# An attention, a router and two dense layers in one kernel: own tiles for the halves of a pair, weight splits moved, the halo of v copied on the chip

## The chip, the core and the metric

The kernel runs as one launch on one core of a Trainium2 chip. The metric is the device time of one execution in microseconds. A core has a matrix engine (TensorE, in the profile PE, its weight loads PEld), a vector engine (VectorE, DVE), a scalar engine (ScalarE, ACT), GpSimd (POOL) and SyncE (SP), which issues most DMA transfers. Each engine takes its instructions strictly in order, and engines wait for one another by semaphores.

## The reference

What is computed, cut to its core (float32 throughout):

```python
# 1. attention: batch 4, 8 heads, 576 positions, 64 per head; window 32.
#    heads 0-3: rel in [0, 32); heads 4-7: rel in [0, 128) and rel % 4 == 0
attn = softmax(where(mask, q @ k.T / 8, -1e9)); x = attn @ v      # -> 2304 x 512
# 2. router: 8 experts of exactly 288 tokens each, greedy by the sorted logits
logits = x @ w_gate                                                # 2304 x 8
out[assigned == e] = relu(x[assigned == e] @ w1[e]) @ w2[e]        # 512 -> 1024 -> 512
# 3. gated layer: 512 -> 1536 -> 512
y = (sigmoid(out @ w_gate2) * (out @ w_val)) @ w_out
```

## The kernel before, in words

The program has four stages, one behind the other on TensorE: the attention, the routing, the eight experts (`phase_m`) and the gated layer (`phase_g`).

**Attention.** The dilated heads are permuted on the host so that they too see a plain window of 32. There are four phases (head kind and batch pair), each of nine blocks of 64 queries: 36 groups, taken two at a time as 18 pairs, here p0 to p17. A block needs its 64 queries, and 96 keys and values: its own 64 and the 32 ahead of them, the halo. The host lays v out with the halo repeated, so that a block of v has 96 rows. `steps` writes the order of the work out by hand. In the turn of pair p stand: loads of the next phase (`load`, on SP's queue), the scores of p (`scores`, TensorE), the transposes of the exponentials of p-1 (`pt`: two halves of four transposes, each half followed by a copy from PSUM on ACT), the router's products of p-3 (`logit`, in the two phases of the plain heads), `norm` and the transposes `xt` of p-2 (DVE, TensorE), the products with v of p-1 (`av`), and the row maximum, subtraction and exponential of p (`soft`: DVE, DVE, ACT). The last pair is taken in halves. The rows of x go to DRAM (`rows_out`, SP). Numbers n in the program count half turns: n = 2p and 2p+1.

Both halves of `pt` write one PSUM tile of two banks and one SBUF tile:

```python
if g == 0:
    self.st[p, "pt"] = (self.ps_t.tile([128, 8, 128], ...), self.sp.tile([KEYS, 8, 128], ...))
...
nc.scalar.copy(t[:, j], ps[0:KEYS, j])
```

**Weights of the experts.** `fetch` loads 512 KB of float32 weights into one of four `raw` buffers. `high` (ACT) rounds them to the upper part, `low` (DVE) subtracts that to get the lower part; both parts lie in a ring of five. The first three splits stand in the attention, at n = 28, 30 and 32, and seven fetches at n = 22 to 25 and 33 to 35.

**Routing.** `settle` searches a threshold for each expert in five steps (DVE and TensorE in turn, with products that keep TensorE busy, `warm`), writes the row numbers (`rows`), starts the gathers of x on GpSimd, and passes a branch on a flag that all engines read. Behind it `tokens` writes `toks`, and the pools of the routing are closed. Then `turn` transposes the gathered rows (tile `xps`), and splits them into `xh` (ACT) and `xl` (DVE); the first product of the experts (tile `hps`) needs both, and the two parts of the weights.

A DMA of SP waits until the eighth DMA ahead of it has landed, so that up to eight are under way.

Of the kernel before, what the change touches and what calls it, by code (L numbers as in the profile page):

```python
# [65 lines left out]
def lay_v(v):  # L66
    a = kinds(v).transpose(0, 1, 5, 2, 3, 4, 6)
    a = np.concatenate([a, np.ones(a.shape[:-1] + (1,), a.dtype)], -1).reshape(2, 2, S, VW)
    a = np.concatenate([np.zeros((2, 2, HALO, VW), a.dtype), a], 2)
    return np.ascontiguousarray(np.stack([a[:, :, QB * i:QB * i + KEYS] for i in range(NBLK)], 3))  # L70


class Attn:
# [3 lines left out]
    def __init__(self, tc, ctx, qh, kh, vh, wgate, cst, xrows, L, LT):  # L77
# [6 lines left out]
        self.ps_s, self.ps_o, self.ps_t, self.ps_x = (p(n, 1, space=PS) for n in ("ps_s", "ps_o", "ps_t", "ps_x"))  # L84
# [10 lines left out]
    def zeros(self, eng):  # L95
        for k in self.k:
            eng.memset(k[:, 0], 0.0)

    def load(self, f, part, what="qkv"):
# [46 lines left out]
    def soft(self, p):  # L146
        nc, V = self.nc, self.nc.vector
        ps = self.st.pop((p, "s"))
        mx = self.sp.tile([128, 2, 4], F32, tag="mx", name="mx")
        d = self.sp.tile([128, 4, 2, KEYS], F32, tag="d", name="d")  # L150
        e = self.sp.tile([128, 8, KEYS], F32, tag="e", name="e")
        for gs in self.halves(p):
            n = 2 * len(gs)
            j = slice(2 * gs[0], 2 * gs[0] + n)
            V.tensor_reduce(out=mx[:, :, j], in_=ps[:, :, j], axis=AX.X, op=ALU.max)
            V.tensor_tensor(out=d[:, j].rearrange("p j h k -> p h j k"), in0=ps[:, :, j],
                            in1=mx[:, :, j].unsqueeze(3).to_broadcast([128, 2, n, KEYS]), op=ALU.subtract)
            nc.scalar.activation(out=e[:, 4 * gs[0]:4 * gs[0] + 2 * n].rearrange("p j k -> p (j k)"), in_=d[:, j].rearrange("p j h k -> p (j h k)"),
                                 func=AF.Exp, scale=0.125)
        self.st[p, "e"] = e  # L160
# [12 lines left out]
    def av(self, p, g):  # L173
        nc = self.nc
        t = self.st[p, "pt"][1]
        if g == 0:
            self.st[p, "o"] = self.ps_o.tile([128, 2, 512], F32, tag="o", name="o")
        o = self.st[p, "o"]
        f, i = self.groups[2 * p + g]
        v = self.v[f % 2][:, i].rearrange("p (b h c) -> p b h c", b=2, h=4)  # L180
        for h in range(4):
            for b in range(2):
                out = slice(64 * b, 64 * b + 64)
                nc.tensor.matmul(o[out, g, 65 * h:65 * h + 65], t[:, 4 * g + h, out], v[:, b, h], start=True, stop=True)

    def norm(self, p, gs=(0, 1)):
        V = self.nc.vector
        o = self.st[p, "o"][:, :, 0:260].rearrange("p g (h c) -> p g h c", h=4)
        if gs[0] == 0:
            self.st[p, "r"] = self.sp.tile([128, 2, 4], F32, tag="r", name="r")  # L190
            self.st[p, "x"] = self.xp.tile([128, 2, 4, 64], F32, tag="x", name="x")
        g = slice(gs[0], gs[-1] + 1)
        r, x = self.st[p, "r"][:, g], self.st[p, "x"][:, g]
        V.tensor_scalar(out=r, in0=o[:, g, :, 64], scalar1=1e-9, scalar2=None, op0=ALU.add)
        V.reciprocal(r, r)
        V.tensor_tensor(out=x, in0=o[:, g, :, 0:64], in1=r.unsqueeze(3).to_broadcast([128, len(gs), 4, 64]), op=ALU.mult)
        for k in gs:
            self.rows_out(2 * p + k, self.st[p, "x"][:, k].rearrange("p h d -> p (h d)"))
# [19 lines left out]
    def xt(self, p, gs=(0, 1)):  # L218
        nc = self.nc
        x = self.st[p, "x"].rearrange("p g (r h) d -> p g r (h d)", r=2)  # L220
        pool, n = (self.ps_t, 1024) if gs == [1] else (self.ps_x, 512)
        ps = pool.tile([128, n], F32, tag="t" if n > 512 else "x", name="xt")[:, 0:512].rearrange("p (r b g q) -> p r b g q", r=2, b=2, g=2)
        for g in gs:
            for r in range(2):
                nc.tensor.transpose(ps[:, r, :, g], x[:, g, r], self.cst["id"])
        self.st[p, "xt", gs[0]] = ps

    def xts(self, p, gs=(0, 1)):
        copy = self.nc.scalar.copy
# [4 lines left out]
        if plain:  # L234
            if (p, "xts") not in self.st:
                self.st[p, "xts"] = self.sp.tile([128, 2, 2, 128], F32, tag="xts", name="xts")
            t = self.st[p, "xts"]
            g = slice(plain[0], plain[-1] + 1)
            copy(t[:, g].rearrange("p g r (b q) -> p (r b) g q", b=2), ps[:, :, :, g].rearrange("p r b g q -> p (r b) g q"))
# [13 lines left out]
    def logit(self, p, gs=(0, 1), out=None):  # L253

        nc = self.nc
        for g in gs:
            f, i = self.groups[2 * p + g]
            kind, bp = self.phases[f]
            if kind:
                continue  # L260
            t, d = self.st[p, "xts"], self.xd
            xs = [t[:, g, r] for r in range(2)] + [d[:, i, r].rearrange("p b j r -> p (b j r)") for r in range(2)]
            j, k = divmod(i, 4)
            for w in (2, 3, 0, 1):
                dst = self.LT[:, 128 * j:128 * j + 128] if out is None else out
                nc.tensor.matmul(dst[32 * w:32 * w + 32], self.wr[:, k, w], xs[w],
                                 start=k == 0, stop=k == 3 or i == NBLK - 1)
# [4 lines left out]
    def fold(self, js):  # L272
        for j in js:
            n = min(4, NBLK - 4 * j)
# [3 lines left out]
    def steps(self):  # L278
        N = len(self.groups) // 2
        A = self.nc.scalar.copy  # L280
        for p in range(N):
# [13 lines left out]
            if p >= 1:  # L295
                self.av(p - 1, 0)
                self.av(p - 1, 1)
            self.soft(p)
            if p >= 2:
                self.xts(p - 2)  # L300
            if p == 12:
                self.spill(slice(0, 384), A)
                self.fold(range(3))
# [27 lines left out]
        self.fold(range(2, 3))  # L331
# [59 lines left out]
class Route:  # L391
# [180 lines left out]
    def settle(self, rows, gather, segments=(5, 1, 2)):  # L572
# [7 lines left out]
        with self.tc.block():  # L580
# [5 lines left out]
            with self.tc.If(v > 0, label="settled"):  # L586
# [3 lines left out]
                gather()  # L590

# [421 lines left out]
def program(tc, top, qh, kh, vh, wgate, cst, csb, wm, wgv, out):  # L1013
    nc = tc.nc
    with tc.manual_schedule():
# [12 lines left out]
        mring = ExitStack()  # L1028
        dn.ring = pool(mring, "ring", 5, side="right")
        with ExitStack() as rt:  # L1030
# [6 lines left out]
            with ExitStack() as at_ctx:  # L1037
# [8 lines left out]
                nc.scalar.activation(out=rows.bitcast(F32)[:, 0:1], in_=nc.const_aps.tensor(1.0, [128, 1], F32), func=AF.Exp)  # L1046
# [89 lines left out]
```

## Time and profile before

| what | value |
|---|---|
| median of three runs | 833.12 us (832.93 to 835.58) |
| the profiled execution's own time | 834.7 us, span 832.9 us |
| attention | 0 to 122.2 us: TensorE busy 90.9 us |
| routing up to `rows` | 122.2 to 156.1 us |
| branch, gather, transposes | 156.1 to 164.7 us |
| experts and gated layer | 164.7 to 832.9 us: TensorE busy 661.6 of 668.2 us |
| DMA share, 0 to 41.5 us | 0.90 of 16 engines, 227 GB/s |

Times of rows count from the span's start. The busy share of TensorE over the span (94%) says little of the attention, where each engine waits for others in every turn. A wait in brackets is the engine's idle time just ahead of the row and what ended it; "issue" there means that no semaphore was waited for.

### The profile page before, as it was taken

Reading aid. Unit: us, or ns where it says so; the run is one execution under the profiler, and the core shown is the slowest. Engines: PE = TensorE matmul, PEld = TensorE weight load, DVE = VectorE, ACT = ScalarE, POOL = GpSimd, SP = SyncE. Lnnn points to the kernel's source line nnn. Section 1 sums busy time; section 2 is a strip of 40 time slices with the busy share of each in tenths; the row PEclk is TensorE's granted clock in tenths of the full one; section 3 lists DMA queues with packets and bytes.
Section 4 is the critical chain, followed back from the end, with each engine's and each line's share of the span. In section 5 each row is a group of like instructions: output and inputs, shape, how many; then the busy total and the mean of one; then the engine's idle time right before and its main releaser. Section 6 shows DMA issues by size and latency. Waiting matters only on the chain.

```text
span 832.9 us, 14224 instructions
## 1 busy us (share of the span) xinstructions
PE 786.3 (94%) x5873; PEld 720.1 (86%) x5873; DVE 436.7 (52%) x747; ACT 303.3 (36%) x534; POOL 49.5 (6%) x72
## 2 busy tenths in 40 slices
PE   8688578799999999999999999999999999999996
PEld 5566454499999999999999999999999999999996
DVE  4455358556677766666654543445655543333322
ACT  3445330155565555544432433332322222212210
POOL 1030000311001100000000000000000000111002
PEclk9899799999999999999999999999999999999999
DMA  9879540256666666535312221112222101121002
GB/s 251 203 222 258 166 144 1 68 167 231 208 242 226 236 235 220 198 111 192 127 48 86 71 79 41 45 45 89 70 65 100 39 20 39 57 76 39 24 14 76
DMA packets 41278, 100.56 MB, mean 121 GB/s; under 512 B 4296, under 2 KB 20328, under 8 KB 41208
## 3 DMA queue, kind: packets, MB, share of 16 engines
q1 hardware_dynamic: 38088, 89.89, 34.2%
q0 software_dynamic: 2976, 9.54, 3.3%
q8 instruction: 48, 0.79, 0.4%
q10 hardware_dynamic: 144, 0.16, 0.1%
q14 instruction: 22, 0.18, 0.1%
HBM read 85.42 MB, written 14.16 MB: 120 GB/s over the span
## 4 chain that ended last, share of the span: by engine, by line
PE 78%; DMA 1%; ACT 1%; DVE 0%; POOLq 0%; POOL 0%; issue 0%; SPq 0%; ACTq 0%
PE gv L923 35%; PE o L945 18%; PE hps L805 12%; PE y L827 12%; PE xps L782 1%; DMA raw<-in_moe_dram 1%; ACT yo L831 0%; ACT L927 0%; POOLq L1132 0%; POOL out_dram L959 0%; DVE acc L957 0%; DVE xl L793 0%; ACT cm L746 0%; ACT xh L792 0%; PE y L847 0%
## 5 line engine op out<-in xcount | busy, mean ns | idle before, releaser
L923 PE MATMUL gv<-yhi,gw 128*128 128x384 f32 x1152 | 305.2, 336 | 0.3 <-ACT sg L927 0.3
L923 PEld LDWEIGHTS gv<-yhi,gw 128*128 128x128 f32 x1152 | 209.3, 188 | 3.7 <-ACT sg L927 0.6
L923 PE MATMUL gv<-ylo,gw 128*128 128x384 f32 x576 | 193.0, 335 | 0.0
L928 DVE TENSOR_TENSOR sg<-sg,gv 128x384 f32<-128x384 f32 x72 | 39.8, 552 | 186.0 <-PE gv L923 186.0
L945 PE MATMUL o<-gw,ghi 128*128 128x512 f32 x432 | 134.4, 392 | 0.0
L923 PEld LDWEIGHTS gv<-ylo,gw 128*128 128x128 f32 x576 | 108.1, 188 | 3.0
L728 DVE TENSOR_TENSOR wlo<-raw,whi 128x1024 fp32r<-128x1024 f32 x64 | 78.3, 1224 | 45.5 <-ACT whi L723 44.9
L931 ACT CAST ghi<-sg 128x384 fp32r<-128x384 f32 x72 | 36.9, 513 | 162.5 <-DVE sg L928 162.5
L945 PEld LDWEIGHTS o<-gw,ghi 128*128 128x128 f32 x432 | 80.1, 188 | 13.4
L927 ACT ACTIVATE sg<-gv 128x384 f32<-128x384 f32 x72 | 35.4, 492 | 144.6 <-PE gv L923 144.3
L945 PE MATMUL o<-gw,glo 128*128 128x512 f32 x216 | 85.4, 396 | 0.0
L805 PE MATMUL hps<-xh,whi 128*128 128x288 f32 x256 | 77.0, 301 | 0.0
L805 PE MATMUL hps<-xh,wlo 128*128 128x288 f32 x256 | 75.9, 297 | 0.0
L827 PE MATMUL y<-hh,wlo 128*128 128x288 f32 x256 | 75.6, 295 | 0.0
L827 PE MATMUL y<-hh,whi 128*128 128x288 f32 x256 | 75.5, 295 | 0.0
L827 PE MATMUL y<-hl,whi 128*128 128x288 f32 x256 | 75.4, 295 | 0.0
L805 PE MATMUL hps<-xl,whi 128*128 128x288 f32 x256 | 75.0, 293 | 0.0
L723 ACT CAST whi<-raw 128x1024 fp32r<-128x1024 f32 x64 | 66.8, 1043 | 8.0 <-DMA raw<-in_moe_dram 8.0
L932 DVE TENSOR_TENSOR glo<-sg,ghi 128x384 fp32r<-128x384 f32 x72 | 40.2, 559 | 41.7 <-ACT ghi L931 41.7
L809 ACT ACTIVATE hh<-hps 128x288 fp32r<-128x288 f32 x64 | 26.4, 412 | 69.8 <-PE hps L805 69.8
L805 PEld LDWEIGHTS hps<-xl,whi 128*128 128x128 f32 x256 | 48.4, 189 | 0.1
L827 PEld LDWEIGHTS y<-hl,whi 128*128 128x128 f32 x256 | 48.4, 189 | 0.0
(139 smaller groups left out, 994.6 us busy)
## 6 DMA issues: line engine op xcount, KB each, us to landing
raw<-in_moe_dram SPq DMA_DIRECT2D x100, 512.0 KB
raw<-yd SPq DMA_DIRECT2D x28, 384.0 KB
v<-in_v_dram SPq DMA_DIRECT2D x12, 390.0 KB
yd<-yo SPq DMA_DIRECT2D x8, 576.0 KB
q<-in_q_dram SPq DMA_DIRECT2D x12, 256.0 KB
k<-in_k_dram SPq DMA_DIRECT2D x12, 256.0 KB
v<-in_v_dram SPq DMA_DIRECT2D x4, 585.0 KB
xrows<-x SPq DMA_DIRECT2D x18, 128.0 KB
```

The source lines that it names most:

```text
L723: self.nc.scalar.copy(hi, self.raw[j])
L728: self.nc.vector.tensor_tensor(out=lo, in0=self.raw.pop(j), in1=hi.bitcast(F32), op=ALU.subtract)
L782: nc.tensor.transpose(ps[:, k], x[:, 128 * k:128 * k + 128], self.ident)
L805: nc.tensor.matmul(ps, w[:, 128 * k:128 * k + 128], x[:, k], start=(n == 0), stop=(n == 11))
L809: nc.scalar.activation(out=hi, in_=ps, func=AF.Relu)
L827: nc.tensor.matmul(y[m], w[:, s], x, start=(f == 0 and n == 0), stop=(f == 7 and n == 2))
L923: nc.tensor.matmul(p, w[:, a, s], x, start=(m == 0), stop=(m == 11))
L927: nc.scalar.activation(out=sg, in_=ps[0], func=AF.Sigmoid)
L928: nc.vector.tensor_tensor(out=sg, in0=sg, in1=ps[1], op=ALU.mult)
L931: nc.scalar.copy(hi, sg)
L932: nc.vector.tensor_tensor(out=lo, in0=sg, in1=hi.bitcast(F32), op=ALU.subtract)
L945: nc.tensor.matmul(self.oa[step][t], x[:, s], w[:, a, 1024:1536], start=(i == 0 and q == 0), stop=(i == FB - 1 and q == 2))
```

## The change

Own tiles: each half of `pt` has a PSUM tile of one bank (two buffers) and an SBUF tile of its own; the exponentials, maxima, and for the last pair the products, norms and transposes, have own tiles too. The last pair's router product is taken directly (`direct`: the transposed rows as weights, eight columns) instead of through the folded form, and the last turns are written in another order. The fold of the first half moves from p12 to behind `av` in p13. The host lays v out without the halo, 64 rows a block; `load` copies 32 rows from one block to the next on GpSimd. The splits of the first three weights move: `high` behind the attention, `low` into `settle`, behind the branch; fetches 0 to 3 move to n = 28 to 31, and fetches 4 to 6 behind the branch. The DMA of the routing's constants moves from n = 4 to n = 10, their spreading on GpSimd from n = 9 on to n = 13 on.

```diff
         if "v" in what:
-            dma(out=self.v[s][:, i0:i1], in_=self.vh[kind, bp, :, i0:i1])
+            v = self.v[s]
+            dma(out=v[HALO:KEYS, i0:i1], in_=self.vh[kind, bp, :, i0:i1])
+            j = min(i1, NBLK - 1)
+            self.nc.gpsimd.tensor_copy(v[0:HALO, i0 + 1:j + 1], v[QB:KEYS, i0:j])
...
     def pt(self, p, g):
         nc = self.nc
-        e = self.st[p, "e"]
-        if g == 0:
-            self.st[p, "pt"] = (self.ps_t.tile([128, 8, 128], F32, tag="t", name="pt"), self.sp.tile([KEYS, 8, 128], F32, tag="pt", name="pts"))
-        ps, t = self.st[p, "pt"]
-        j = slice(4 * g, 4 * g + 4)
-        for i in range(4 * g, 4 * g + 4):
+        e = self.st.pop((p, "e", g))
+        ps = self.ps_t.tile([128, 4, 128], F32, tag="t", name="pt")
+        t = self.sp.tile([KEYS, 4, 128], F32, tag=f"pt{g}", name="pts")
+        for i in range(4):
             nc.tensor.transpose(ps[0:KEYS, i], e[:, i], self.cst["id"])
-        nc.scalar.copy(t[:, j], ps[0:KEYS, j])
+        nc.scalar.copy(t, ps[0:KEYS])
+        self.st[p, "pt", g] = t
...
+    def direct(self, p, g):
+        i = self.groups[2 * p + g][1]
+        for w, x in enumerate(self.terms(p, g)):
+            self.nc.tensor.matmul(self.L[:, i], x, self.wg[:, w], start=w == 0, stop=w == 3)
...
         m = N - 1
-        self.logit(m - 2)
         self.pt(m, 0)
         self.norm(m - 1)
+        self.pt(m, 1)
+        self.logit(m - 2)
         self.xt(m - 1)
-        self.pt(m, 1)
         yield 2 * N
         self.av(m, 0)
-        self.norm(m, [0])
         self.xts(m - 1)
         self.av(m, 1)
+        self.norm(m, [0])
         self.norm(m, [1])
+        self.logit(m - 1, NBLK - 3)
+        self.spill(slice(0, 256), A)
+        yield 2 * N + 1
         self.xt(m, [0])
-        yield 2 * N + 1
-        self.logit(m - 1)
-        self.xts(m, [0])
+        self.xts(m, [0], A)
         self.xt(m, [1])
-        self.logit(m, [0])
-        self.xts(m, [1])
+        self.xts(m, [1], nc.vector.tensor_copy)
+        self.fold(range(2), NBLK - 2)
         yield 2 * N + 2
-        self.spill(slice(0, 256), A)
-        last = self.ps_s.tile([128, 2, 512], F32, tag="s", name="sc")[:, 0, 0:128]
-        self.logit(m, [1], last)
-        self.fold(range(2))
-        self.nc.vector.tensor_copy(self.lts[:, 256:384], last)
-        self.fold(range(2, 3))
+        self.direct(m, 0)
+        self.direct(m, 1)
...
-                    if n in (28, 30, 32):
-                        dn.high(n // 2 - 14)
-                        dn.low(n // 2 - 14)
-                    if n in (33, 34, 35):
-                        dn.fetch(n - 29)
+                    if n in (28, 29, 30, 31):
+                        dn.fetch(n - 28)
...
+            for j in range(AHEAD):
+                dn.high(j)
...
+            def fill():
+                for j in range(AHEAD):
+                    dn.low(j)
+                    dn.fetch(j + 4)
```

Three places show how the order of the instructions changes. The first is TensorE in the turn of p2: `pt` is the PSUM tile of the transposes, `e` the exponentials, `o` the products with v, and `DMAHW`, `DVE`, `Activation`, `Pool` and `PE` are semaphores. Before:

```order
L170 MATMUL pt<-ident,e 96x128 [waits PE_49,Activation_49]
L170 MATMUL pt<-ident,e 96x128 x3
L170 MATMUL pt<-ident,e 96x128 [waits Activation_49]
L170 MATMUL pt<-ident,e 96x128 x3
L225 MATMUL xt<-ident,x 128x2x64 [waits DVE_49]
L225 MATMUL xt<-ident,x 128x2x64 x3
L184 MATMUL o<-v_141,pts 64x65 [waits DMAHW6_49,PE_49]
L184 MATMUL o<-v_141,pts 64x65 x7
L184 MATMUL o<-v_141,pts 64x65 [waits Activation_49]
L184 MATMUL o<-v_141,pts 64x65 x7
```

After:

```order
L172 MATMUL pt<-ident,e 96x128 [waits PE_49,Activation_49]
L172 MATMUL pt<-ident,e 96x128 x3
L172 MATMUL pt<-ident,e 96x128 [waits PE_49]
L172 MATMUL pt<-ident,e 96x128 x3
L231 MATMUL xt<-ident,x 128x2x64 [waits DVE_49]
L231 MATMUL xt<-ident,x 128x2x64 x3
L190 MATMUL o<-v_138,pts 64x65 [waits DMAHW6_49,Activation_49]
L190 MATMUL o<-v_138,pts 64x65 x7
L190 MATMUL o<-v_138,pts 64x65 [waits Activation_49,Pool_49]
L190 MATMUL o<-v_138,pts 64x65 x7
```

The second half of the transposes no longer waits for ACT; the products with v now wait for both copies themselves, and those of the second group for GpSimd, which has copied the halo.

The second place is ACT. Before, in the turns of p14 and p15, the cast `whi` of a weight stands between the exponential `e` of one pair and the copy `pts` of the next:

```order
L158 ACTIVATE e<-d 128x768 [waits DVE_49,Activation_49]
L249 COPY xd<-xt 128x4x3x16 [waits PE_49]
L249 COPY xd<-xt 128x4x5x16
L723 CAST whi<-raw 128x1024 [waits DMAHW0_49]
L171 COPY pts<-pt 96x512 [waits PE_49,Activation_49]
L171 COPY pts<-pt 96x512 [waits PE_49]
L158 ACTIVATE e<-d 128x768 [waits DVE_49,Activation_49]
```

After, from the copies of the last pair on, the three casts stand behind the last copy of the attention, ahead of the routing's branch:

```order
L173 COPY pts<-pt 96x512 [waits PE_49] x2
L243 COPY xts<-xt 128x4x2x64 [waits PE_49,Activation_49]
L281 COPY lts<-L 128x256 [waits PE_49]
L243 COPY xts<-xt 128x256 [waits PE_49]
L734 CAST whi<-raw 128x1024 [waits DMAHW2_49]
L734 CAST whi<-raw 128x1024 [waits DMAHW3_49]
L734 CAST whi<-raw 128x1024 [waits DMAHW7_49]
L590 UNCONDITIONAL_BRANCH
```

The casts have left the turns of the attention and run where ACT has nothing else to do until the routing's branch.

The third place is DVE at the end of the routing: `rows` are the gathered rows' numbers, `xl` the lower part of the first gathered rows. Before:

```order
L558 SCALAR_TENSOR_TENSOR rows_69<-pip_104 128x18 [waits DMASW4_49,DMASW5_49,DMASW3_49,DVE_49]
L586 UNCONDITIONAL_BRANCH
L586 UNCONDITIONAL_BRANCH [waits DVE_49,DVE_sequencer_49]
L563 TENSOR_SCALAR ib_2467<-pip_104 128x18 [waits DVE_49]
L564 TENSOR_SCALAR ib_2467<-pip_104 128x18
L565 TENSOR_TENSOR ib_2467<-ib_2467 128x18 [waits DVE_49]
L566 SCALAR_TENSOR_TENSOR ib_2467<-pip_104 128x18 [waits DVE_49]
L567 TENSOR_TENSOR toks_70<-ib_2467 128x18 [waits DVE_49]
L793 TENSOR_TENSOR xl_2513<-xps_2507,xh_2512 128x4x128 [waits Activation_49]
```

After:

```order
L568 SCALAR_TENSOR_TENSOR rows_69<-pip_101 128x18 [waits DMASW4_49,DMASW5_49,DMASW3_49,DVE_49]
L596 UNCONDITIONAL_BRANCH
L596 UNCONDITIONAL_BRANCH [waits DVE_49,DVE_sequencer_49]
L739 TENSOR_TENSOR wlo_1779<-raw_1401,whi_1778 128x1024 [waits DMAHW2_49,Activation_49]
L739 TENSOR_TENSOR wlo_1782<-raw_1404,whi_1781 128x1024 [waits DMAHW3_49,Activation_49]
L739 TENSOR_TENSOR wlo_1785<-raw_1482,whi_1784 128x1024 [waits DMAHW7_49,Activation_49]
L573 TENSOR_SCALAR ib_2525<-pip_101 128x18 [waits DVE_49]
L574 TENSOR_SCALAR ib_2525<-pip_101 128x18
L575 TENSOR_TENSOR ib_2525<-ib_2525 128x18 [waits DVE_49]
L576 SCALAR_TENSOR_TENSOR ib_2525<-pip_101 128x18 [waits DVE_49]
L577 TENSOR_TENSOR toks_70<-ib_2525 128x18 [waits DVE_49]
L804 TENSOR_TENSOR xl_2571<-xps_2565,xh_2570 128x4x128 [waits Activation_49]
```

The three subtractions `wlo` now stand behind the branch and ahead of the five instructions that end in `toks`.

## Rows read from the trace of the kernel before

**Rows 1.** The chain that ended last, in order of time: start us, us, what.
```profile
164.73 5.03 PE hps L805 x36
```

**Rows 2.** Waits of PE, whole span: us in total, times, longest us.
```profile
PE pt L170 <- ACT pts L171: 20.8, 18, 8.5
...
PE L L275 <- ACT lts L270: 1.2, 1, 1.2
```

**Rows 3.** PE timeline, 25 to 44 us: start, length, instruction [idle before, releaser].
```profile
25.68 0.55 PE L134 MATMUL sc<-k,q 64*64 64x96 f32 x12 [1.39 <-issue]
...
30.56 0.64 PE L170 MATMUL pt<-ident,e 128*96 128x128 f32 x4
31.93 0.64 PE L170 MATMUL pt<-ident,e 128*96 128x128 f32 x4 [0.73 <-ACT pts L171]
32.41 0.60 PE L225 MATMUL xt<-ident,x 128*128 128x128 f32 x4
...
36.12 0.59 PE L184 MATMUL o<-v,pts 96*64 96x65 f32 x12 [2.38 <-issue]
36.64 0.53 PE L127 MATMUL sc<-cb 64*64 64x384 bf16 x4
...
43.74 0.36 PE L127 MATMUL sc<-cb 64*64 64x384 bf16 x4
```

**Rows 4.** DMA queues between 33.0 and 33.5 us: packets, MB, share.
```profile
q8 instruction: 1, 0.02, 17.7%
```

**Rows 5.** Windows: stretch, busy PE, PEld, DVE, ACT, POOL, PEclk, DMA share, GB/s.
```profile
38.00:40.00 2.00, 1.48 (x16) 0.81 (x8) 1.36 (x2) 0.43 (x1) 0.00 (x0) 0.50 0.19 60
122.20:156.10 33.90, 26.37 (x196) 15.04 (x195) 26.93 (x95) 0.56 (x1) 1.35 (x1) 0.95 0.00 1
```

**Rows 6.** PE timeline, p14 to p17.
```profile
80.00 0.36 PE L127 MATMUL sc<-cb 64*64 64x384 bf16 x4
...
84.72 0.36 PE L127 MATMUL sc<-cb 64*64 64x384 bf16 x4
...
94.85 1.09 PE L170 MATMUL pt<-ident,e 128*96 128x128 f32 x4 [8.54 <-ACT pts L171]
...
99.71 0.54 PE L127 MATMUL sc<-cb 64*64 64x384 bf16 x4
...
105.55 0.36 PE L127 MATMUL sc<-cb 64*64 64x384 bf16 x4
```

**Rows 7.** ACT timeline, the long wait of p15.
```profile
93.27 1.04 ACT L723 CAST whi<-raw 128x1024 fp32r<-128x1024 f32 x1 [7.98 <-DMA raw<-in_moe_dram]
```

**Rows 8.** DVE timeline, pair p5.
```profile
31.82 0.96 DVE L156 TENSOR_TENSOR d<-sc,mx 128x768 f32<-128x768 f32 x1
```

**Rows 9.** PE timeline, end of the attention.
```profile
108.39 0.64 PE L170 MATMUL pt<-ident,e 128*96 128x128 f32 x4 [1.25 <-ACT pts L171]
...
110.95 0.63 PE L225 MATMUL xt<-ident,x 128*128 128x128 f32 x4 [1.35 <-DVE x L196]
...
114.00 0.30 PE L266 MATMUL L<-xts,wr 128*32 128x128 f32 x2 [1.00 <-ACT xts L239]
...
118.31 0.69 PE L184 MATMUL o<-v,pts 96*64 96x65 f32 x16 [1.12 <-DVE x L196]
...
121.27 0.83 PE L275 MATMUL L<-fold,lts 128*128 128x32 f32 x6
```

**Rows 10.** PE timeline, from the end of the routing to the experts.
```profile
156.34 4.49 PE L443 MATMUL L<-const-bfloat16-1.0 128*128 128x512 bf16 x13 [2.02 <-DVE rows L558]
161.38 0.63 PE L782 MATMUL xps<-ident,xg 128*128 128x128 f32 x4 [0.56 <-DVE toks L567]
```

**Rows 11.** DVE timeline: a lower part, and the end of the routing.
```profile
94.34 1.23 DVE L728 TENSOR_TENSOR wlo<-raw,whi 128x1024 fp32r<-128x1024 f32 x1 [11.24 <-ACT whi L723]
...
160.49 0.22 DVE L563 TENSOR_SCALAR ib<-pip 128x18 f32<-128x18 f32 x1 [4.39 <-DVEq L586]
```

**Rows 12.** GpSimd (POOL) timeline, 40 to 48 us.
```profile
40.38 7.45 POOL L434 COPY rtab<-rc 128x288 bf16<-128x288 bf16 x20 [30.09 <-DMA rc<-in_small_dram]
```

More of the change, by code (lines that the diff above doesn't have):

```diff
@@ L97, in zeros @@
             eng.memset(k[:, 0], 0.0)
+        for v in self.v:
+            eng.memset(v[0:HALO, 0], 0.0)
     def load(self, f, part, what="qkv"):
@@ L148, in soft @@
         ps = self.st.pop((p, "s"))
-        mx = self.sp.tile([128, 2, 4], F32, tag="mx", name="mx")
-        d = self.sp.tile([128, 4, 2, KEYS], F32, tag="d", name="d")
-        e = self.sp.tile([128, 8, KEYS], F32, tag="e", name="e")
         for gs in self.halves(p):
-            n = 2 * len(gs)
+            n, t = 2 * len(gs), "" if len(gs) > 1 else str(gs[0])
             j = slice(2 * gs[0], 2 * gs[0] + n)
[L155 to L159, printed above, removed]
@@ L160, in soft @@
-        self.st[p, "e"] = e
+            mx = self.sp.tile([128, 2, n], F32, tag="mx" + t, name="mx")
+            d = self.sp.tile([128, n, 2, KEYS], F32, tag="d", name="d")
+            e = self.sp.tile([128, 2 * n, KEYS], F32, tag="e", name="e")
+            V.tensor_reduce(out=mx, in_=ps[:, :, j], axis=AX.X, op=ALU.max)
+            V.tensor_tensor(out=d.rearrange("p j h k -> p h j k"), in0=ps[:, :, j],
+                            in1=mx.unsqueeze(3).to_broadcast([128, 2, n, KEYS]), op=ALU.subtract)
@@ L162, in pt @@
+            nc.scalar.activation(out=e.rearrange("p j k -> p (j k)"), in_=d.rearrange("p j h k -> p (j h k)"), func=AF.Exp, scale=0.125)
+            for k, g in enumerate(gs):
+                self.st[p, "e", g] = e[:, 4 * k:4 * k + 4]
     def pt(self, p, g):
         nc = self.nc
-        e = self.st[p, "e"]
-        if g == 0:
-            self.st[p, "pt"] = (self.ps_t.tile([128, 8, 128], F32, tag="t", name="pt"), self.sp.tile([KEYS, 8, 128], F32, tag="pt", name="pts"))
-        ps, t = self.st[p, "pt"]
@@ L174, in av @@
         nc = self.nc
[L175 to L178, printed above, removed]
+        t = self.st.pop((p, "pt", g))
+        if g in [gs[0] for gs in self.halves(p)]:
+            pool, tag = (self.ps_s, "s") if g else (self.ps_o, "o")
+            o = pool.tile([128, 2, 512], F32, tag=tag, name="o")
+        else:
+            o = self.st[p, "o", 0]
+        self.st[p, "o", g] = o
         f, i = self.groups[2 * p + g]
@@ L234, in xts @@
         if plain:
-            if (p, "xts") not in self.st:
-                self.st[p, "xts"] = self.sp.tile([128, 2, 2, 128], F32, tag="xts", name="xts")
-            t = self.st[p, "xts"]
+            t = self.sp.tile([128, len(plain), 2, 128], F32, tag=f"xts{len(plain)}", name="xts")
             g = slice(plain[0], plain[-1] + 1)
-            copy(t[:, g].rearrange("p g r (b q) -> p (r b) g q", b=2), ps[:, :, :, g].rearrange("p r b g q -> p (r b) g q"))
+            copy(t.rearrange("p g r (b q) -> p (r b) g q", b=2), ps[:, :, :, g].rearrange("p r b g q -> p (r b) g q"))
+            for k, g in enumerate(plain):
+                self.st[p, "xts", g] = t[:, k]
         if perm:
@@ L251, in xts, with terms, logit, fold @@
                 a += n_
-    def logit(self, p, gs=(0, 1), out=None):
-        nc = self.nc
-        for g in gs:
+    def terms(self, p, g):
+        t, i = self.st.pop((p, "xts", g)), self.groups[2 * p + g][1]
+        return [t[:, r] for r in range(2)] + [self.xd[:, i, r].rearrange("p b j r -> p (b j r)") for r in range(2)]
+    def logit(self, p, last=NBLK - 1):
+        for g in range(2):
             f, i = self.groups[2 * p + g]
-            kind, bp = self.phases[f]
-            if kind:
+            if self.phases[f][0]:
                 continue
-            t, d = self.st[p, "xts"], self.xd
-            xs = [t[:, g, r] for r in range(2)] + [d[:, i, r].rearrange("p b j r -> p (b j r)") for r in range(2)]
+            xs = self.terms(p, g)
             j, k = divmod(i, 4)
             for w in (2, 3, 0, 1):
-                dst = self.LT[:, 128 * j:128 * j + 128] if out is None else out
-                nc.tensor.matmul(dst[32 * w:32 * w + 32], self.wr[:, k, w], xs[w],
-                                 start=k == 0, stop=k == 3 or i == NBLK - 1)
+                self.nc.tensor.matmul(self.LT[32 * w:32 * w + 32, 128 * j:128 * j + 128], self.wr[:, k, w], xs[w],
+                                      start=k == 0, stop=k == 3 or i == last)
+    def direct(self, p, g):
+        i = self.groups[2 * p + g][1]
+        for w, x in enumerate(self.terms(p, g)):
+            self.nc.tensor.matmul(self.L[:, i], x, self.wg[:, w], start=w == 0, stop=w == 3)
     def spill(self, c, copy):
         copy(self.lts[:, c], self.LT[:, c])
-    def fold(self, js):
+    def fold(self, js, blocks=NBLK):
         for j in js:
-            n = min(4, NBLK - 4 * j)
+            n = min(4, blocks - 4 * j)
             self.nc.tensor.matmul(self.L[:, 4 * j:4 * j + n].rearrange("p c e -> p (c e)"), self.lts[:, 128 * j:128 * j + 128],
@@ L279, in steps @@
         N = len(self.groups) // 2
-        A = self.nc.scalar.copy
+        nc = self.nc
+        A = nc.scalar.copy
         for p in range(N):
@@ L297, in steps @@
                 self.av(p - 1, 1)
+            if p == 13:
+                self.fold(range(3))
             self.soft(p)
@@ L302, in steps @@
                 self.spill(slice(0, 384), A)
-                self.fold(range(3))
             yield 2 * p
@@ L570, in load_flag, with settle @@
         return self.nc.values_load(self.flag[0:1, 0:1], min_val=0, max_val=64)
-    def settle(self, rows, gather, segments=(5, 1, 2)):
+    def settle(self, rows, gather, fill, segments=(5, 1, 2)):
         s = 0
@@ L590, in settle @@
                 gather()
+        fill()
     def more(self, s, segments):
```

57 lines of the change are left out of this document (27 added, 30 removed).

## The prediction

> **What bounds the kernel now.** I read the chain of work that ended last first. It goes back without a break to 164.73 us, the first product of the experts [rows 1]; from there TensorE is the bound, and the change touches nothing that it waits for. So whatever the change brings is the amount by which that first product moves. Ahead of it stand attention and routing, and there I read the waits of TensorE: 20.8 us in 18 waits of the transposes `pt` for ACT's copy `pts` [rows 2], the longest 8.5 us. The timeline shows what the usual one is. In p5 the first half of `pt` starts at 30.56, the second at 31.93, having waited for the copy of the first half, and the next product 0.48 us later [rows 3]. The second half writes another bank and reads other exponentials; it waits because the tile is one.
>
> Three other losses are to be seen. TensorE stops at 25.68 (1.39 us) and 36.12 (2.38 us) in the middle of a series, waiting for no semaphore [rows 3]. Just ahead of the second, between 33.0 and 33.5, an instruction block of 0.02 MB goes through a DMA queue [rows 4]; I read both holes as instructions that came late behind the loads of q, k and v. [...] The largest loss is p15: 14.99 us against 4.72 of p14, with 8.54 us of wait [rows 6], because ACT sat 7.98 us on a cast `whi` for its weight from DRAM [rows 7], and the copy `pts` is queued behind that cast.
>
> **The change part by part.** Own tiles for the halves. Without the wait the second half follows at the pitch of 0.48 instead of 1.37 us: 0.89 a pair. I take 0.85, since `av` now waits for the copies itself. In p1, where nothing stands between `pt` and `av`, I take 0.5. p2 to p16 are 15 pairs: 12.75 + 0.5 = **13.25 us**. What is late next? DVE: in p5 its subtraction ends at 32.78 [rows 8]. The next scores, which overwrite its source, start at 36.64, or 34.26 without the hole of 2.38 [rows 3], and now 0.85 earlier, at 33.4. That leaves 0.6 us, so DVE doesn't become the bound, but it is near. Bounds: nothing, if the inputs set the pace (a rival), and 15 x 0.89 + 0.5 = 13.9.
>
> Weight splits out of the attention. p15 loses 14.99 - 4.72 = 10.3 us of hole and slow clock, p16 5.84 - 4.72 = 1.1 [rows 6]: **11.4 us**. The casts run on ACT in the routing, which uses it 0.56 of 33.9 us [rows 5]; three casts of 1.04 [rows 7] are covered. Without that cover they would cost 3.1 us.
>
> Fold behind `av`. The wait of 1.2 us for the copy `lts` [rows 2] goes; that copy now stands ahead of p12's `pts` on ACT, for which I keep back 0.2: **1.0 us**.
>
> End of the attention. TensorE waits there 1.25, 1.35, 1.00 and 1.12 us [rows 9]. The first is the shared tile; the second is `norm` behind a lower part `wlo` on DVE; the third goes because `logit` comes later, behind both `pt`; the fourth is the product tile shared by the two groups. Together 4.7 us. The last group's chain (norm, transposes, copy, products) stays. `direct` has eight products of two passes; the nearest row is the fold's six passes in 0.83 us [rows 9], so 16 passes are 2.2 us. They replace the last two groups' folded products, a copy and one fold; I count that as equal. I take **4.6 us**; bounds 3 (a new wait of 1.6 in that chain) and 6 (eight columns go faster than 32).
>
> Lower parts behind the branch. This costs. The branch leaves DVE at 160.49, then come the five instructions of `toks` [rows 11], and the first transposes `xps` of the experts wait for exactly those (0.56 us, at 161.38) [rows 10]. Now three `wlo` of 1.23 us [rows 11], three times 1.22 as their starts follow one another, stand ahead of `toks`. Queued behind them are `toks`, `xl`, and on TensorE all of the experts: **-3.7 us**. The stretch in which DVE waited 4.39 us for the branch [rows 11] can't hide them, since they stand behind it. TensorE's filler products end at 160.83, so it then idles about 4.2 us. Those fillers, 13 in 4.49 us behind a wait of 2.02 [rows 10], show how slow it is after such a gap; for the slower first transposes I take **-0.5 us** (bounds 0 and 2). Fetches 4 to 6 are issued behind one `wlo` each, at about 162 to 164 on this scale; the cast of block 4 comes when three blocks have been multiplied, which takes 5.03 us [rows 1], so at about 173. That covers the transfers, and I cost them at nothing; a rival has it otherwise.
>
> Halo on GpSimd. v is a third smaller, and 16 copies of 32 x 1040 are added. The nearest row spreads 288 bf16 elements in 7.45 / 20 = 0.37 us [rows 12]: by elements 1.35 us, by bytes 2.7. A phase has four copies, 5 to 11 us in a stretch of about 17, and like its loads they run ahead of their use by some pairs. Nothing on the path. GpSimd's spreading of the constants queues among them and has until the end of the attention. The DMA of the constants leaves the early stretch. The smaller loads shorten the wait of the instruction blocks about as much as TensorE comes earlier, so I leave both holes and the slow p6 as they are: 0 (bounds: +3.8 for the holes, +2.4 for p6, which is 7.10 against p14's 4.72).
>
> More such holes. Between the two holes lie 10.4 us [rows 3] and 124 products. With shorter pairs such a block is used up about 1.1 us sooner, and the loads of the last phase and of the weights may fill the DMA as those did. I take one new hole as long as the smaller one: **-1.5 us** (bounds 0 and -5). [...]
>
> **Sum.** 13.25 + 11.4 + 1.0 + 4.6 = 30.25 gained, 3.7 + 0.5 + 1.5 = 5.7 lost: 24.55 us. Against the profiled execution's own 834.7: 810.15. The median of the runs shown, 833.12, is 1.6 lower, so 808.5 us.
>
> **Rivals.** Holes closed. Smaller loads and a steadier TensorE close both holes, p6 runs at full clock, none is added: 3.8 + 2.4 + 1.5 = 7.7 better, 800.8. For it: 1.2 MB less ahead of the second hole (a seventh of the q, k and v of two phases, by the shapes). Against: TensorE asks for its blocks sooner too.
>
> Lower parts hidden. The pool of the transposes might not wait for `toks`: 4.2 better, 804.3. Against: that wait [rows 10].
>
> Weights late. Fetches 4 to 6 start some 50 us later than now and share the DMA with the gathers; TensorE waits about 4 us at the third or fourth block: 812.5.
>
> Inputs set the pace. Loads, stores in one in-order queue and instruction blocks keep the pairs at their old length: the 13.25 are lost, and no new hole counts: 834.7 - 12.8 - 1.6 = 820.3. For it: the holes. Against: 20.8 us of waits for `pts` [rows 2] stand against 3.8 of holes.
>
> Slower: GpSimd becomes the bound. Every second `av` waits for a copy of the halo. The forecast ends the attention at 122.2 - 30.25 + 1.5 = 93.5; with about 10 us ahead of the first copy and 14 behind the last, 70 us remain for the 16, an estimate. So they bind from 4.4 us each, and from 6.1 (27 us more) the kernel is slower by over 0.3%, which is about what a measurement here can tell from no change. That is 4.5 times the price by elements; only a very bad shift from partitions 64 to 0 would do it.
>
> **How the numbers follow.** Forecast 0.54, holes closed 0.14, lower parts hidden 0.07, weights late 0.08, inputs 0.12, GpSimd 0.04, no effect 0.01. The range of 800 to 818 holds the first four, 0.83, with the bounds of the single terms. Faster 0.95, same 0.01, slower 0.04.
>
> **What would show it.** Right: no wait of `pt` for `pts` from p1 to p16, pairs shorter by 0.85 us, p15 like its neighbours; no `whi` in the attention; its last product at 92 to 95 us; the first `xps` 43 us behind that product, where it is 39.3 now (122.1 to 161.38), waiting for `toks`. Wrong: idle of TensorE ahead of `o` put down to POOL; pairs that keep their length, with waits on DVE, loads or "issue"; `hps` waiting for a cast of block 4. What would undo the forecast most is the pairs' new length, 13.25 of the 24.55 us.

## The result and the profile after

The changed kernel takes 801.46 us in the median of 4 runs (801.04 to 801.83), the one before 833.02 (829.00 to 835.58): ratio 0.9625, 95% interval 0.9586 to 0.9664. The time lies in the range forecast, near its lower end. The profiled execution's span is 799.9 us, 33.0 less than before; of these, 1.7 are because the profiled execution of before, 834.7 us, lies above its median.

TensorE's timeline after, at the starts of p5 to p7, of p15 and p17, and at the one hole that is left:

```profile
23.85 0.36 PE L131 MATMUL sc<-cb 64*64 64x384 bf16 x4
27.33 0.36 PE L131 MATMUL sc<-cb 64*64 64x384 bf16 x4
30.82 0.36 PE L131 MATMUL sc<-cb 64*64 64x384 bf16 x4
...
43.89 0.33 PE L190 MATMUL o<-v,pts 96*64 96x65 f32 x3 [0.68 <-issue]
...
64.22 0.36 PE L131 MATMUL sc<-cb 64*64 64x384 bf16 x4
...
71.69 0.36 PE L131 MATMUL sc<-cb 64*64 64x384 bf16 x4
```

Against [rows 3, 6]: p6 starts at 27.33 and not 36.64, and takes 3.49 us and not 7.10; p15 and p16 together take 7.47 and not 20.83. No `pt` waits for `pts`. The rest of the way, on VectorE, from the first reduction of the last logits on:

```profile
84.11 0.23 DVE L463 TENSOR_REDUCE rm<-L 128x9 f32<-128x72 f32 x1 [2.32 <-PE L L278]
...
120.10 0.18 DVE L568 SCALAR_TENSOR_TENSOR rows<-pip 128x18 int32<-128x18 f32 x1
...
124.36 3.50 DVE L739 TENSOR_TENSOR wlo<-raw,whi 128x1024 fp32r<-128x1024 f32 x3 [4.08 <-DVEq L596]
...
128.60 1.28 DVE L804 TENSOR_TENSOR xl<-xps,xh 128x512 fp32r<-128x512 f32 x2
```

and on TensorE at the change from routing to experts:

```profile
125.61 0.63 PE L793 MATMUL xps<-ident,xg 128*128 128x128 f32 x4 [0.56 <-DVE wlo L739]
...
129.34 0.65 PE L793 MATMUL xps<-ident,xg 128*128 128x128 f32 x4 [1.91 <-DVE xl L804]
...
136.87 0.30 PE L838 MATMUL y<-hh,whi 128*128 128x288 f32 x1
```

The first `xps` comes 5.3 us behind `rows` here as before (120.28 to 125.61; 156.10 to 161.38), though three `wlo` now stand where the five instructions up to `toks` did, and `toks` ends only at 128.69: so it waits for neither `toks` nor the last two `wlo`. In both kernels it comes 4.3 to 4.4 us behind the issue of its gather (157.11 and 121.20), and 4.4 us in `e9_x8_lows` below, where the `wlo` stand elsewhere. That it waits for its gathered rows is the reading that fits; no wait in the traces names them. The third `xps` is what waits for the `wlo`, through `xl`, and behind that wait the first products run slowly, as two rows of the same shape show:

```profile
131.32 0.44 PE L816 MATMUL hps<-xh,whi 128*128 128x288 f32 x1
...
134.09 0.29 PE L816 MATMUL hps<-xh,whi 128*128 128x288 f32 x1
```

Two windows around the routing's start (TensorE's granted clock is the number behind the counts, then DMA share and GB/s):

```profile
82.00:84.00 2.00, 2.00 (x15) 1.96 (x15) 0.00 (x0) 1.15 (x2) 0.00 (x0) 0.68 0.85 301
...
88.00:90.00 2.00, 1.78 (x8) 0.84 (x8) 2.00 (x11) 0.00 (x0) 0.00 (x0) 0.50 0.00 0
```

The granted clock falls to 0.50 during the direct products, at about 82.7 us, and comes back to 1.00 at about 93.0 us; before the change it was 1.00 at this place (104 to 124 us). All that the routing loses is lost there: from the third row of six fillers on, before

```profile
135.91 2.72 PE L443 MATMUL L<-const-bfloat16-1.0 128*128 128x512 bf16 x6
```

and after

```profile
100.10 2.72 PE L453 MATMUL L<-const-bfloat16-1.0 128*128 128x512 bf16 x6
```

it is 20.2 us to the end of `rows` in both; from the first reduction to this row it is 13.7 us before and 16.0 after.

By stretches, profile against profile, forecast in brackets: up to p6's start +9.3 (3.9); p6 +3.6 (0.85); p7 to p14 +7.6 (6.3); p15 and p16 +13.4 (13.1); the attention's end from p17's start +4.2 (4.6); routing -2.3 (0); `rows` to the first `y` product of the experts -3.1 (-4.2); the rest +0.3. The first two are 8.2 us above the forecast; the others nearly cancel to the 8.4 of the sum.

What differs there is the DMA. Its share and rate in 40 slices from 5 to 30 us, before:

```profile
DMA  8999999999999999999999999999999999999999
GB/s 243 357 261 213 188 265 251 256 344 377 224 217 235 310 336 410 308 189 176 199 224 263 204 320 255 175 204 257 276 257 252 182 201 224 240 270 282 220 195 207
```

and after:

```profile
DMA  9999999999999999999999999744342122221122
GB/s 397 294 366 381 403 405 401 400 428 439 399 382 384 406 387 400 409 368 403 408 390 402 372 389 443 290 153 160 112 136 77 33 67 84 90 77 48 46 61 80
```

The DMA engines are as busy, but before the change the rate drops again and again to 175 to 250 GB/s, and after it stays near 400 until the loads are done. The last load of the first two phases is issued at 25.42 us before and at 17.08 after, for a seventh fewer bytes. The experiments ask why.

### The profile page after: what moved, and what is told of

Its sections match the earlier page's. It is cut to its first block, busy times and chain, and to the rows that moved or that the text cites. A ratio compares the mean times of both kernels' runs of the same rounds, so it can differ in the third digit from the quotient of the medians.

```text
span 799.9 us, 14280 instructions
## 1 busy us (share of the span) xinstructions
PE 781.2 (98%) x5871; PEld 720.4 (90%) x5871; DVE 437.6 (55%) x749; ACT 303.0 (38%) x533; POOL 66.3 (8%) x88
## 4 chain that ended last, share of the span: by engine, by line
PE 82%; DMA 1%; DVE 1%; ACT 1%; issue 0%; POOLq 0%; POOL 0%; SPq 0%; DVEq 0%
PE gv L934 37%; PE o L956 19%; PE hps L816 13%; PE y L838 13%; PE xps L793 1%; DMA raw<-in_moe_dram 1%; DVE wlo L739 0%; ACT yo L842 0%; ACT L938 0%; POOLq L1145 0%; POOL out_dram L970 0%; DVE acc L968 0%; ACT cm L757 0%; DVE xl L804 0%; PE y L858 0%
## 5 line engine op out<-in xcount | busy, mean ns | idle before, releaser
L956 PEld LDWEIGHTS o<-gw,ghi 128*128 128x128 f32 x432 | 80.1, 188 | 13.4
L970 POOL DMA_INDIRECT out_dram<-acc,toks x18 | 17.5, 972 | 502.5 <-DVE acc L968 475.2
```

The costliest lines, as they stand in the source:

```text
L956: nc.tensor.matmul(self.oa[step][t], x[:, s], w[:, a, 1024:1536], start=(i == 0 and q == 0), stop=(i == FB - 1 and q == 2))
L970: st = nc.gpsimd.indirect_dma_start(out=self.out, out_offset=bass.IndirectOffsetOnAxis(ap=self.toks[:, c:c + 1], axis=0), in_=acc, in_offs ...
```

## The experiments

Times are medians; each stands beside runs of the kernel before on the same chip (831.6 to 832.3). "After" is 801.46, and was measured beside 833.02, so a difference to it of 1 to 2 us says nothing by itself. Edits are shown shortened, `...` and comments standing for what is left out.

**Values undone: `e1_v96`.**

```
-   dma(out=v[HALO:KEYS, i0:i1], in_=self.vh[kind, bp, :, i0:i1])
-   self.nc.gpsimd.tensor_copy(v[0:HALO, i0 + 1:j + 1], v[QB:KEYS, i0:j])
+   dma(out=self.v[s][:, i0:i1], in_=self.vh[kind, bp, :, i0:i1])   # vh of 96 rows
```

> The kernel after, but the values' part alone undone: v comes again as 96 rows in one transfer, without the GpSimd copies. Theory S (the transfer of 96 rows by its shape runs at about 240 GB/s where 64 rows ran at 380 to 403 GB/s, and the inputs' loads up to 26 us delayed the first pairs): the 5 to 20 us stretch falls back to 230 to 310 GB/s at a DMA share of 1, the loads of the first two phases end their issue near 25 us and not 17.6, the two early holes of 1.4 and 2.4 us and the slow sixth pair come back, and the kernel takes 806 to 810 us. Rival B (only the bytes: 96 rows are 14% more in the first two phases): the rate stays near 380 GB/s, issue ends near 20 us, 802 to 804 us. Rival P (the holes went with the pairs' waits, not with the loads): the rate may fall, but no hole comes back and the time stays at 801 to 802 us.

825.19 us (822.31 to 827.49), ratio 0.9895 (0.9854 to 0.9935): the small part of the change is worth 23.7 us, some three times what theory S had. The rate falls as it said (5 to 20 us), and the last load of the first two phases is issued at 25.72:

```profile
5.00:20.00 15.00, 13.35 (x269) 9.96 (x269) 8.12 (x13) 5.62 (x8) 1.10 (x7) 1.00 1.04 268
```

The holes come back, but not as the two of before: 0.88 us ahead of 16.97 and 3.48 ahead of 26.99, and the slow pair is p4 (10.33 us, 22.15 to 32.48), while p6 takes 3.48. The longest waits of TensorE up to 125 us, of which the kernel after has only 0.60 us of `xt` for `x` and one hole of 0.68:

```profile
PE xt L227 <- DVE x L197: 4.4, 3, 2.9
PE xt L227 <- issue: 3.8, 1, 3.8
PE sc L134 <- DMA k<-in_k_dram: 3.6, 4, 2.7
PE sc L134 <- issue: 3.5, 1, 3.5
```

With shorter pairs the slow loads are missed later on too: 2.72 us for `k` ahead of 54.81, and `x` waits 1.95, 2.33 and 2.67 us until an earlier pair's store, in the same queue as the loads, has read its buffer. This is the rival "inputs set the pace", kept away by the values' part alone. Rivals B and P fall.

**The same bytes in two transfers: `e2_v64_32`.** As above, but rows 32 to 95 and rows 0 to 31 apart:

```
+   for a, b in ((32, 96), (0, 32)):
+       dma(out=self.v[s][a:b, i0:i1], in_=self.vh[kind, bp, a:b, i0:i1])
```

> The same bytes as the undone values' part, but each load as two transfers, 64 rows and the 32 rows of the halo, still without GpSimd copies. Theory S: the shape of 96 rows is what was slow, so the rate stays near 380 GB/s in 5 to 20 us, no early hole, 801 to 804 us. Rival B (bytes): like the 96-row run, within 1 us of it. Rival P: 801 to 802 us whatever the rate.

817.96 us (815.35 to 820.08), 309 GB/s from 5 to 20 us: between the two. No theory had this. What suggests itself is where the rows go: 64 rows to partitions 32 to 95 were fast, 32 rows to 0 to 31 and 96 rows to 0 to 95 perhaps not. The next pair tries that.

**Only the place changed: `e8_rows0` and `e8_rows32`.** One more load of the same 64 rows into an unread tile `du`, behind each values' load of the first two phases:

```
+   if f < 2:
+       dma(out=self.du[s][0:64, i0:i1], in_=self.vh[kind, bp, :, i0:i1])   # or [32:96, ...]
```

> The kernel after, with one more transfer behind each load of values of the first two phases: the same 64 rows again, into a tile that nobody reads, on partitions 0 to 63. Its pair puts the same rows on partitions 32 to 95, and nothing else differs. Theory P (where the rows lie decides the rate: 96 rows on 0 to 95, and 32 rows on 0 to 31, load one half of SBUF's partitions more than the other, while 32 to 95 lies evenly over both): while the extra rows load the rate falls to some 200 to 250 GB/s at a DMA share of 1, the loads' issue ends 5 us or more later than in its pair, and the kernel takes 5 us or more longer than its pair. Rival C (the count of rows or their bytes decide, 64 rows being as good anywhere): both kernels alike, near 390 GB/s, within 1 us of each other.

> The same extra 64 rows, on partitions 32 to 95. Theory P: 380 to 400 GB/s throughout, the loads' issue ends some 6 us later than in the kernel after (2.34 MB more at 390 GB/s), and the kernel takes 801 to 806 us, by how far the third and fourth parts were early. Rival C: as its pair, whatever that is.

819.20 us (818.51 to 825.65) on partitions 0 to 63, 811.45 (810.05 to 812.63) on 32 to 95: 7.75 us between kernels that differ in a partition number. The window of 20 to 25 us in the first:

```profile
20.00:25.00 5.00, 3.06 (x71) 2.45 (x69) 2.53 (x5) 2.86 (x5) 2.74 (x7) 1.00 1.04 280
```

and in the second:

```profile
20.00:25.00 5.00, 4.68 (x115) 4.04 (x115) 3.26 (x7) 3.68 (x7) 1.90 (x3) 1.00 1.03 396
```

So the place of the rows sets the rate here: up to 36 us, eight of the first kernel's 40 slices of 0.9 us fall to 181 to 217 GB/s at a DMA share of 0.9 or more, while in the second none lies below 337 from 2.7 us until its loads are done at 27. Theory P had 5 us or more for the pair, and it was 7.75; its reason wasn't tried apart, and no run shows why 0 to 63 is the slower place. Nor is the place all of it: `e1_v96` and `e2_v64_32` put the same rows on the same partitions, and the second is 7.2 us faster. How a load is cut counts too; no run shows why.

The second kernel was 10.0 us slower than after and 5 us over its expectation, though its rate stayed near 400. TensorE waits 2.3 us for `k`, and the last `x` waits for a store, as in its pair (4.63 us) and in the two kernels above (2.67, 5.83); in the kernel after it is 0.40:

```profile
90.62 0.42 DVE L204 TENSOR_TENSOR x<-o,r 128x256 f32<-128x256 f32 x1 [5.47 <-DMA xrows<-x]
```

So these bytes cost time at near 400 GB/s too, and how the 23.7 us divide between the halo's bytes, their place and the cut isn't shown.

**Values alone: `e7_before_v`,** the kernel before with:

```
-   dma(out=self.v[s][:, i0:i1], in_=self.vh[kind, bp, :, i0:i1])
+   dma(out=v[HALO:KEYS, i0:i1], in_=self.vh[kind, bp, :, i0:i1])
+   self.nc.gpsimd.tensor_copy(v[0:HALO, i0 + 1:j + 1], v[QB:KEYS, i0:j])
```

> The kernel before with the values' part of the change alone (64 rows loaded, halo copied by GpSimd, the three constants' loads issued ahead of the copies). Theory S: the loads are issued by about 18 us, both early holes and the slow sixth pair go, 7 to 9 us gained against before: 824 to 827 us. Rival B: 1 to 2 us gained. Rival P (holes go only when the pairs' waits go): within 1 us of before, 832 to 834 us.

820.64 us (820.28 to 821.29): 11.4 gained, more than theory S. The starts of p7, p15 and p17:

```profile
36.60 0.36 PE L131 MATMUL sc<-cb 64*64 64x384 bf16 x4
...
77.60 0.36 PE L131 MATMUL sc<-cb 64*64 64x384 bf16 x4
...
91.44 0.53 PE L131 MATMUL sc<-cb 64*64 64x384 bf16 x4
```

p7 starts at 36.60 instead of 43.74, which is both early holes and the slow p6; p15 and p16 give as much again (13.8 us instead of 20.8). The two profiles are 14.4 us apart, the medians 11.4, because the profiled execution of before lies 2.7 above the median used here. So values alone give 11.4, and values on top of the rest 23.7: the parts don't add. The constants of the routing are loaded at their old place here, so moving them isn't what closes the holes; three small loads are issued ahead of the copies, as in the kernel after.

**Shared transposes: `e3_shared`.**

```
-   ps = self.ps_t.tile([128, 4, 128], F32, tag="t", name="pt")
-   t = self.sp.tile([KEYS, 4, 128], F32, tag=f"pt{g}", name="pts")
+   if g == 0: self.st[p, "pt"] = (ps_t.tile([128, 8, 128]), sp.tile([KEYS, 8, 128]))
```

> The kernel after, but the two halves of the transposed exponentials share one tile in PSUM and one in SBUF again, as before the change. Theory W (the term of the forecast: 0.85 us of PE wait in each of the pairs 1 to 16): TensorE waits on ACT's pts again, about 16 times 0.85 us, and the kernel takes 813 to 816 us, the early pairs included now that inputs do not hold them. Rival R (the wait is only exchanged for another at a pair's next step, ACT's or VectorE's): waits on pts appear but the pair grows by under 0.3 us, 802 to 806 us.

815.52 us (813.12 to 817.87), 14.1 more, as the forecast's term had it. The wait is back:

```profile
PE pt L174 <- ACT pts L175: 12.9, 18, 0.7
```

**Splits back: `e4_splits_back`.**

```
+   if n in range(22, 26): dn.fetch(n - 22)
+   if n in (28, 30, 32):
+       dn.high(n // 2 - 14)
+       dn.low(n // 2 - 14)
+   if n in (33, 34, 35): dn.fetch(n - 29)
```

> The kernel after, with the first three weights' upper and lower parts back inside the attention (steps 28, 30 and 32) and the six fetches where they were. Theory D (the forecast's term: the upper parts in ACT's queue hold the pairs' exponentials while their weights are on the way, 11.4 us for the three, less the 3.7 us that the lower parts behind the branch cost): 8 to 12 us slower than the kernel after, 809 to 813 us, with a wait of ACT for raw of several us near pair 14. Rival E (with faster inputs the weights come in time): the wait for raw is under 2 us, the splits cost only their 3 times 1.05 us on ACT and 3 times 1.2 us on VectorE in part, 801 to 805 us.

810.13 us (808.14 to 811.18), 8.7 more; forecast was 11.4 - 3.7 = 7.7 for the two terms. p15 and p16 take 15.4 us together (65.32 to 80.75). But ACT's wait for a weight is only 1.36 us now. The loss sits on VectorE, where `x` is queued behind a lower part that waits for its upper part:

```profile
69.42 1.33 DVE L739 TENSOR_TENSOR wlo<-raw,whi 128x1024 fp32r<-128x1024 f32 x1 [4.36 <-ACT whi L734]
```

and on TensorE:

```profile
71.94 1.08 PE L231 MATMUL xt<-ident,x 128*128 128x128 f32 x4 [4.60 <-DVE x L201]
```

TensorE's `xt` waits 4.60 us for that `x`. The size held; the wait had passed from ACT's copies to VectorE.

**Lower parts and clock: `e5_lows_in_routing`, `e6_warm`.** The first moves the lower parts, in `update`; the second adds fillers of 254 columns, in `steps`:

```
+   for j in {0: (0,), 1: (1, 2)}.get(s, ()):     # e5, ahead of V.tensor_scalar(out=self.ok, ...)
+       dn.low(j); dn.fetch(j + 4)
...
+   self.warm(5)                                  # e6, ahead of self.xt(m, [1])
...
    self.direct(m, 0)
+   self.warm(3)                                  # e6
    self.direct(m, 1)
```

> The kernel after, with the three lower parts of the first weights moved from behind the branch into the routing: one ahead of VectorE's wait for TensorE in the first update (1.47 us idle there), two in the second (2.11 us). Theory L (the two xl copies that wait behind the three lower parts and the tokens set the start of the first layer): the third xps waits no more, the first hps starts some 2.5 us after the first xps and not 4.7, and 2.0 to 2.8 us are gained. Rival G (the gathers set it: the third was issued 2.65 us behind the first): the third xps waits for its rows, 1.0 to 1.3 us gained. Rival N (the lower parts hold VectorE in the routing as long as they did behind it): within 0.5 us of the kernel after.

> The kernel after, with eight more filler products of 254 columns in the attention's tail: five in TensorE's wait ahead of the last x transposes, three between the two blocks of direct products. Theory K (the clock fell to 0.50 at 82.4 us after the wait and the products of 8 columns, and the slow clock cost the routing 2.3 us): the granted clock stays 1.00 from 82 to 93 us, VectorE's first two waits for the counts shrink from 1.47 and 2.11 us to under 1 us each, and 1.4 to 2.3 us are gained less up to 0.4 us that the fillers take. Rival M (the clock falls all the same, or a little later): 0.3 to 0.6 us lost.

803.93 us (801.34 to 804.75) and 805.97 (805.22 to 809.14). Neither gains; the second is worse than after, the first can hardly be told from it (ratio to before 0.9655, 0.9633 to 0.9678, against 0.9625, 0.9586 to 0.9664). Both traces show the same new loss, here that of the second run (0.40 us in the kernel after, 2.66 in the first run):

```profile
86.31 0.42 DVE L201 TENSOR_TENSOR x<-o,r 128x256 f32<-128x256 f32 x1 [4.98 <-DMA xrows<-x]
```

`x` has five buffers (the last pair, in two tiles since the change, takes one more than before), and an earlier pair's store, queued on SyncE among the weights' fetches, hadn't read its buffer yet. In the first run `rows` to `y` took 14.7 us, 1.9 less than after, and that was lost to this wait; in the second the clock fell anyway while TensorE stood still (0.56 from 84 to 86 us, in which no product ran), so theory K isn't tried by it.

**With eight buffers: `e9_x8_lows`, `e10_x8_lows_warm`.** With e5's lower parts, and in the second with e6's fillers too:

```
-   self.xp, self.sp = p("ax", 5), p("as", 2)
+   self.xp, self.sp = p("ax", 8), p("as", 2)
```

> The run with the lower parts in the routing, and eight buffers instead of five for the attention's normalised results x. Theory X (that run lost its gain because VectorE's last x waited 2.7 us for an earlier x's stores, which the weights' fetches had pushed back; the lower parts themselves gained about 1.9 us between rows and the first product of the second layer): no wait of x on its stores, the attention ends as early as in the kernel after or up to 1 us earlier, and the time is 798.0 to 799.8 us. Rival Y (the stores set the pace in another way, or the lower parts made that wait): 801 to 804 us again, with the tail of the attention as long as there.

> The same, with the eight filler products in the attention's tail. Theory K (now without the wait of 4.5 us on x that let TensorE stand still in the first trial of the fillers): the granted clock stays 1.00 for most of 82 to 93 us and the routing from its first reduction to rows shrinks from 36.1 to 34 us or less; 0.8 to 2 us faster than its pair without fillers. Rival M (the products of 8 columns let the clock fall whatever stands around them): the clock falls to 0.50 again near 82 us, 0 to 0.6 us slower than its pair.

799.63 us (798.22 to 802.74), ratio to before 0.9618 (0.9595 to 0.9642), and 800.33 (799.71 to 802.16), ratio 0.9625 (0.9604 to 0.9646). No `x` waits for a store any more: theory X holds. `rows` to `y` shrinks to 13.4 and 13.6 us, but of that 3 us little arrives: in the first the routing grew from 36.2 to 37.1 (three `wlo` don't quite fit the waits), and p17 starts at 73.59 and 74.18 instead of 71.69, with instruction holes of 0.77 and 1.59 us where the kernel after has 0.68. Fillers hold the clock at first (its pair without them has 0.67 from 84 to 86 us):

```profile
82.00:90.00 8.00, 6.99 (x72) 5.45 (x63) 4.99 (x16) 3.68 (x5) 0.00 (x0) 1.00 0.52 187
```

but at about 91.3 us it falls all the same, to 0.50 for some 3 us. The routing takes 35.8 us, 1.3 less than in its pair and not the 34 of theory K; the tail is 0.35 us longer by the fillers and the hole 0.8. So the pair stands at 799.63 and 800.33, and neither can be told from the kernel after.

**Everything in the tail: `e12_tail`.** Fetches at steps 26 to 29, `high(0)` behind the last but one `xts`, `low(0)`, `low(1)` ahead of the last `take`, `low(2)` in the first update, the fillers; five buffers for `x`, as in the kernel after:

```
+   if n in (26, 27, 28, 29): dn.fetch(n - 26)
...
    self.xts(m - 1)
+   dn.high(0)
...
+   dn.high(1); dn.high(2)
+   dn.low(0); dn.fetch(4); dn.low(1); dn.fetch(5)
    r.take(1)
```

> The kernel after, with its five buffers for x, but the first four fetches two to three steps earlier (26 to 29), the first upper part in ACT's wait ahead of the logits' spill, two lower parts in VectorE's wait for the direct products, the third in the first update's, and the eight filler products. Theory Z (what the single trials showed adds up: 3.1 us from the lower parts, with their place now in waits of the attention's tail instead of the routing, some 1.3 us from the clock, and no wait of x on its stores, since the fetches are over before the last pairs' stores): rows to the first product of the second layer 13.5 to 14 us, routing 34 to 35 us, no wait of x over 0.5 us, 796 to 798.5 us. Rival Q (the fetches at steps 26 to 29 hold the stores of the pairs before instead, or the weights' parts hold the tail): the attention's end comes 1 to 4 us later than the 12.4 us from the last pair's start, 799 to 803 us.

806.57 us (801.98 to 807.34): theory Z falls. `x` waits for its stores again, 1.28 and 3.26 us, with the fetches two steps earlier, and the attention's end comes late (89.4 us, against 84.1 after). So earlier fetches don't take that wait away; eight buffers did.

## Why the prediction was right, and where its sizes were off

Of the signs named, no `pt` waits, p15 is like its neighbours and no `whi` stands in the turns of the pairs. The attention's last product ends at 84.0 and not at 92 to 95, and the first `xps` starts 41.6 us behind it and not 43.

**Own tiles, 13.25.** Right: p7 to p14 get 7.6 us shorter together, no `pt` waits, and sharing the tile again costs 14.1.

**Splits, 11.4 and 1.0 for the fold.** Right in size: 13.4 for p15 and p16, which also lost two pairs' waits of 0.85. But the 11.4 isn't the splits' alone: in `e7_before_v` the values take 7.0 us out of these two pairs with the splits where they were, and putting the splits back into the kernel after costs them 8.0 (7.47 to 15.43).

**Attention's end, 4.6.** 4.2; a new wait of 0.60 us of `xt` for `x`, itself held by a store, is the difference.

**Lower parts behind the branch, -3.7 and -0.5.** The loss is 3.1, by another way. The step that failed is "the first transposes `xps` of the experts wait for exactly those": the first starts 3.1 us ahead of the end of `toks` now, and the profile only put its wait down to `toks`. The price comes a step later: 1.6 us at the third `xps`, and 1.5 at the first `hps` products, which run at the low clock (0.52 from 132 to 134 us). With the lower parts elsewhere it is gone (13.4 us instead of 16.6).

**Early holes and p6, 0.** This is the mis-sized term: "I leave both holes and the slow p6 as they are: 0 (bounds: +3.8 for the holes, +2.4 for p6 ...". It measured +8.2, above even its bounds (0.6 of it lies ahead of p1), and so the rival "holes closed" told the first 30 us better than the forecast. That the other errors nearly cancel, 2.3 us lost in the routing against 1.3 gained on p7 to p14 and 1.1 on the lower parts, is luck. I had costed the smaller loads by their bytes, a seventh. They also came faster, 392 GB/s where it was 265 (5 to 20 us), in which the place of the rows may have a part (7.75 us for the same 64 rows), and the rate column of the profile before held the clue: low rates at a full DMA share. Taking GpSimd's copies for the part without weight was the error; alone they give 11.4 us, and without them 23.7 are lost.

**New holes, -1.5.** One, 0.68 us, under half of my term. With the slow loads back, holes of 3.5 and 3.8 us were there again; that the loads delay the instruction blocks is the reading that fits, but no run changed the blocks alone.

**Missing: the routing, -2.3.** I let the clock out at the end of the attention. With three lower parts inside the routing, fillers there gave back 1.3 us of it (37.1 to 35.8) and made the tail 0.35 longer, and the median doesn't show a gain; how much they give without those lower parts, no run shows.

**GpSimd as the bound.** A copy takes 1.04 us, less than the price by elements (1.35), and no `o` waits for it.

## What to carry over

Read the DMA's rate beside its busy share: here a share of 0.9 at some 200 GB/s, where other loads came at near 400, pointed to the shape or the place of a transfer, and copies of 1.04 us on the chip were better than the last rows of it. Parts of a change on one path don't add; undo each in the new kernel and try it alone in the old. Before filling an engine's idle time in a tail, see which buffers wait for stores in the same queue: three trials here (`e5`, `e6`, `e12`) lost there what they were to win.

## What the hardware showed unexpectedly

The same 64 rows loaded to partitions 0 to 63 instead of 32 to 95 cost 7.75 us over eight loads, with the rate down from near 400 to about 200 GB/s in eight slices of 0.9 us while the DMA engines stayed busy. With 96 rows on 0 to 95 (`e1_v96`) 19 of the 40 slices up to 30 us lay at 199 to 250 GB/s with the engines as busy, and the same 96 rows in two transfers were 7.2 us faster.
